# Transpositions of q and k as 64-row tiles, half-size loads, and a new instruction order in an attention and gated-MLP kernel

## The chip, the cores and the metric

The kernel runs on one core of a Trainium2 chip. The metric is the device time in microseconds. Three runs of the kernel before took 740.59, 742.3 and 740.95 us; the median is 740.95 us. Smaller is better.

The engines are TensorE (PE, its weight loads shown apart as PEld), VectorE (DVE), ScalarE (ACT), GpSimd (POOL) and SyncE (SP, which here issues nearly all DMAs). A line number such as L526 is a line of the kernel before.

## What is computed

An attention with hashed buckets, followed by a gated MLP with a spatial gate. Everything is float32.

```python
B, H, S, D = q.shape                       # 4, 8, 768, 64
q_bits = (einsum('bhsd,dk->bhsk', q, proj) > 0)        # 6 bits each, for q and k
mask = q_bucket[:, :, :, None] == k_bucket[:, :, None, :]
scores = where(mask, scale * q @ k.T, -1e9)
attn = exp(scores - max(scores)); attn /= sum(attn) + 1e-9
x = (attn @ v) as (B, S, H*D)              # 4 x 768 x 512
h = gelu(x @ w_in)                         # 512 -> 1024
u, v = halves of h;  v_n = layernorm(v) * g_ln
v_s = w_sg @ v_n + b_sg                    # 768 x 768 over positions
out = x + (u * v_s) @ w_out
```

## The kernel before, in words

Two heads of one batch form a pair; there are 16 pairs. The attention of a pair is done with both heads side by side on the 128 partitions: head 0 on partitions 0 to 63, head 1 on 64 to 127. For that q and k must stand transposed, with the 64 features on the partitions and the 768 positions along the row.

For each pair the work is this:

- `load` (L502) issues, from SP's queue, two DMAs for q and two for k, one for each head, 192 KB each. They put 128 positions on the partitions, in six blocks. The tiles `q` and `k` have one buffer each, so a pair's load waits until the pair before has been read.
- `parts` (L519) transposes: `tr` (L523) makes six TensorE transpositions of 128x128 into two PSUM banks for q, and six for k. ScalarE copies the result back over the same tile (L536), makes the rounded high part `hq`, `hk` (L530), and VectorE the low part `lq`, `lk` (L533).
- `features` (L546) projects q and k on the six hash vectors (L553). VectorE takes the signs (`fc`, L556), and four DMAs from SP (L569) scatter them into `fq` and `fk`.
- `largest` (L573) computes, for six tiles of queries, approximate masked scores in 24 pairs of matmuls (L584), and VectorE takes the row maxima (L589). `shift` (L592) spreads the maxima with three small matmuls (L602) and writes them into `fq` (L608).
- `weigh` (L612) computes the exact scores, four terms each (L624), and ScalarE takes the exponential `p` (L629). GpSimd adds the exponentials up (L642).
- `weighted` (L645) multiplies by v (L654), and sums the denominators (L678).

The matmuls of L584 and L624 take 64 rows and 128 columns each, two at a time: one head on the upper 64 rows of the array, the other on the lower. The transpositions take all 128 rows.

The second part of the program, the gated MLP (L845, L876, L894, L923), comes after the last pair. Beside the attention run the conversion of its weights (L379 to L389) and other preparations.

The order of all instructions is set by the class `Plan`. Every piece of work is added with an engine, a cost and a priority (`add`, L99), and `order` (L129) plays a list schedule with these numbers. The priorities come from constants at the top (L22 to L49). Each engine then runs its list strictly in that order. `form` tells the planner which shape the array has for a piece; `TURN_PE` is what it charges for a change of shape.

Of the kernel before, what the change touches and what calls it, by code (L numbers as in the profile page):

```python
# [14 lines left out]
AF = mybir.ActivationFunctionType  # L15
ALU = mybir.AluOpType
# [5 lines left out]
MLP = {"xl": "POOL", "gm": "DVE", "gl": "POOL", "wg": 450.84, "wo": 131.34, "x": 480}  # L22
# [3 lines left out]
HID = 308.55  # L26
AVP = 3.07
S0P = -1.32
AHEAD = 4
PREP, SHIFTP, FINP, WSTEP, WP = 8.92, -3.65, 6.26, 37.69, 29.58  # L30
LOADS = "SP"
GPLACE = 4
XLATE = 7.75
FEAT = 2.17
LOWP = 7.32
LOADP = -0.4
LATF = 3.2
# [11 lines left out]
ADDW = 1  # L49


class Plan:
# [23 lines left out]
    def __init__(self):  # L76
        self.groups, self.tags = [], {}
# [21 lines left out]
    def add(self, engine, cost, prio, fn, r=(), w=(), dma=0, port=None, form=None, lat=0.0):  # L99

        port = engine == "POOL" if port is None else port
        g = {"e": engine, "c": cost, "p": prio, "fn": fn, "dma": dma, "n": len(self.groups), "slots": [], "port": port, "form": form, "lat": lat}
# [163 lines left out]
def kernel(  # L266
# [190 lines left out]
    if True:  # L457
# [44 lines left out]
        def load(n, prio):  # L502
# [16 lines left out]
        def parts(st, s, prio):  # L519
# [15 lines left out]
            plan.add(PE, 0.654, prio, tr, [raw], [tp])  # L535
            plan.add(ACT, 0.81, prio, lambda: nc.scalar.copy(x_of(raw).rearrange("p (a b) -> p a b", a=2), tp()[:, :, :SH]), [tp], [raw])  # L536
            def split(p1, p2):
                plan.add(ACT, 0.81, p1 + OH[s], high, [raw], [hh])
                plan.add(DVE, 0.98, p2 + OL[s], low, [raw, hh], [lo], port=True)
# [6 lines left out]
        def features(st, prio, merged=False):  # L546
# [13 lines left out]
            else:  # L560
                plan.add(PE, 0.66, prio, project, st.raw, [fp], form="col32")
            st.sign = lambda prio: plan.add(DVE, 0.56, prio, sign, [fp], [fc])
# [10 lines left out]
        def largest(st, t, prio):  # L573
# [13 lines left out]
            for kh in range(2):  # L587
                plan.add(PE, 0.346, prio + 0.01 * kh + OM[2 * t + kh], lambda kh=kh: mm(kh), [*st.hi, *st.ft], [sc[kh]], form="row")
                plan.add(DVE, 0.95, prio + OM[2 * t + kh], lambda kh=kh: nc.vector.tensor_reduce(  # L589
                    mx()[:, i, :, kh], sc[kh]()[:, :, :SH], axis=AX.X, op=ALU.max, negate=True), [sc[kh]], [(mx, (kh, i))])  # L590

        def shift(st, hf, prio):  # L592
# [5 lines left out]
                m()[:, :, MROW::BL], mx(), axis=AX.X, op=ALU.min), [mx], [m])  # L598
# [5 lines left out]
            plan.add(PE, 0.18, prio, spread, [m], [tp])  # L604
            ft, cs = st.ft[0], slice(hf * SH, (hf + 1) * SH)
            for b in range(2):
                r = b * BL + MROW
                plan.add(ACT, 0.47, prio, lambda r=r: nc.scalar.copy(ft()[r:r + 1, cs], tp()[r:r + 1, :SH]), [tp], [(ft, hf)])  # L608
# [3 lines left out]
        def weigh(st, hf, k0, prio):  # L612
# [13 lines left out]
            for i, kt in enumerate(kts):  # L626
                plan.add(PE, 0.692, prio + 0.01 * i + OW[HT * 2 * hf + kt], lambda i=i: mm(i), [qh, ql, kh, kl, kf, (qf, hf)], [sc[i]], form="row")
                ticks.append(plan.buf("tick", 1000))
                plan.add(ACT, 0.81, prio, lambda i=i: nc.scalar.activation(p[i]()[:, :, :SH], sc[i]()[:, :, :SH], AF.Exp),  # L629
                         [sc[i]], [p[i], ticks[-1]])  # L630

            st.p += p
            for i, kt in enumerate(kts):
# [6 lines left out]
                else:  # L640
                    for j in range(2):
                        plan.add(POOL, 1.03, prio + 0.6, lambda i=i, j=j, first=first: nc.gpsimd.tensor_add(  # L642
                            sums()[:, j], (first or sums)()[:, j, :SH], p[i]()[:, j, :SH]), [p[i]] + ([first] if first else []), [(sums, j)])

        def weighted(st, hf, prio, owed, nxt=None):  # L645
# [12 lines left out]
            else:  # L658
# [8 lines left out]
                plan.add(PE, 1.3 * HT, prio - 0.01, product, p + [v_], [av], form="col")  # L667
# [318 lines left out]
```

## Time and profile before

| | |
|---|---|
| median of three runs | 740.95 us |
| profiled execution, its own time | 739.75 us |
| span of the profiled execution | 738.0 us |
| PE busy | 717.1 us (97%) |
| DVE busy | 544.0 us (74%) |
| POOL busy | 459.8 us (62%) |
| ACT busy | 379.5 us (51%) |

The page counts a matmul as busy from its start to its modelled end. Matmuls overlap, so busy time of PE says little on how full it is; the steps from one start to the next say more. The attention takes the span from about 25 to 426 us, the gated MLP the rest.

### The profile page before, as it was taken

Reading aid. Unit: us, or ns where it says so; the run is one execution under the profiler, and the core shown is the slowest. Engines: PE = TensorE matmul, PEld = TensorE weight load, DVE = VectorE, ACT = ScalarE, POOL = GpSimd, SP = SyncE. Lnnn points to the kernel's source line nnn. Section 1 sums busy time; section 2 is a strip of 40 time slices with the busy share of each in tenths; the row PEclk is TensorE's granted clock in tenths of the full one; section 3 lists DMA queues with packets and bytes.
Section 4 is the critical chain, followed back from the end, with each engine's and each line's share of the span. In section 5 each row is a group of like instructions: output and inputs, shape, how many; then the busy total and the mean of one; then the engine's idle time right before and its main releaser. Section 6 shows DMA issues by size and latency. Waiting matters only on the chain.

```text
span 738.0 us, 14443 instructions
## 1 busy us (share of the span) xinstructions
PE 717.1 (97%) x5300; PEld 566.5 (77%) x5300; DVE 544.0 (74%) x859; ACT 379.5 (51%) x623; POOL 459.8 (62%) x465
## 2 busy tenths in 40 slices
PE   6899999999999999999999999999999999999997
PEld 5676676666767666676766669998999889988996
DVE  3887899788898888878788878655864486347733
ACT  3565566665757656565765556530761066106510
POOL 2578889889887878778597976570463045404230
PEclk8999999999999999999999999999999999999999
DMA  6214543653675464255343235935220601061004
GB/s 139 70 45 103 127 114 90 154 132 94 155 143 123 93 149 108 70 128 125 96 108 95 73 85 135 239 68 139 34 64 23 157 15 43 1 147 25 1 1 115
DMA packets 180839, 70.59 MB, mean 96 GB/s; under 512 B 158112, under 2 KB 170528, under 8 KB 180768
## 3 DMA queue, kind: packets, MB, share of 16 engines
q1 hardware_dynamic: 180320, 69.01, 39.3%
q10 hardware_dynamic: 448, 0.66, 0.6%
q8 instruction: 42, 0.69, 0.4%
q14 instruction: 29, 0.24, 0.1%
HBM read 51.61 MB, written 17.24 MB: 93 GB/s over the span
## 4 chain that ended last, share of the span: by engine, by line
PE 76%; DMA 10%; DVE 9%; SPq 2%; issue 2%; ACT 1%; POOL 0%; DVEq 0%; ACTq 0%
PE psb L624 15%; PE psb L654 13%; PE psb L894 11%; PE psb L923 9%; PE psb L845 8%; PE psb L876 7%; PE psb L584 7%; DVE mx L589 4%; DMA r<-sq 2%; PE psb L526 2%; DMA rs<-r 2%; PE psb L678 1%; PE psb L553 1%; DMA sq<-s 1%; PE psb L602 1%
## 5 line engine op out<-in xcount | busy, mean ns | idle before, releaser
L642 POOL TENSOR_TENSOR sum<-sum,p 128x384 f32<-128x384 f32 x256 | 240.7, 977 | 54.8 <-ACT p L629 54.7
L589 DVE TENSOR_REDUCE mx<-psb 128x2 f32<-128x768 f32 x192 | 174.2, 950 | 39.7 <-PE psb L584 39.2
L629 ACT ACTIVATE p<-psb 128x768 f32<-128x768 f32 x192 | 147.1, 815 | 24.3 <-PE psb L624 20.8
L654 PE MATMUL psb<-p,v 128*64 128x385 f32 x768 | 131.2, 491 | 0.0
L654 PEld LDWEIGHTS psb<-p,v 128*64 128x64 f32 x768 | 52.3, 137 | 71.7 <-issue 62.4
L642 POOL TENSOR_TENSOR sum<-p,p 128x384 f32<-128x384 f32 x64 | 71.2, 1133 | 19.5 <-ACT p L629 19.5
L624 PE MATMUL psb<-hq,hk 64*128 64x384 f32 x384 | 72.0, 370 | 5.3 <-DVE mx L589 5.1
L584 PE MATMUL psb<-fk,fq 64*128 64x384 f32 x384 | 68.8, 353 | 2.3 <-DVE mx L589 2.3
L855 POOL TENSOR_TENSOR mv<-mv,epsr 128x1 f32<-128x1 f32 x24 | 13.8, 574 | 86.4 <-DVE mv L854 81.2
L584 PE MATMUL psb<-hk,hq 64*128 64x384 f32 x384 | 66.0, 339 | 0.0
L624 PE MATMUL psb<-lq,hk 64*128 64x384 f32 x384 | 64.9, 333 | 0.0
L624 PE MATMUL psb<-fq,fk 64*128 64x384 f32 x384 | 64.9, 332 | 0.0
L624 PE MATMUL psb<-hq,lk 64*128 64x384 f32 x384 | 64.8, 332 | 0.0
L894 PE MATMUL psb<-wgl,zh 128*128 128x384 f32 x192 | 64.2, 335 | 0.4 <-POOL wgl L817 0.4
L894 PE MATMUL psb<-wgh,zh 128*128 128x384 f32 x192 | 64.1, 334 | 0.0
L894 PE MATMUL psb<-wgh,zl 128*128 128x384 f32 x192 | 64.1, 334 | 0.0
L905 POOL TENSOR_TENSOR gs<-gt,gs 128x384 fp32r<-128x384 f32 x32 | 33.6, 1056 | 48.9 <-ACT gs L902 45.6
L669 ACT COPY un<-psb 128x385 f32<-128x385 f32 x32 | 15.4, 482 | 94.1 <-PE psb L654 94.1
L829 ACT ACTIVATE h<-psb 128x384 f32<-128x384 f32 (+1 forms) x56 | 29.4, 535 | 66.8 <-PE psb L845 59.9
L923 PE MATMUL psb<-woh,gs 128*128 128x512 f32 x192 | 59.9, 389 | 0.0
L897 DVE TENSOR_TENSOR gt<-psb,b_bc 128x384 f32<-128x384 f32 x32 | 17.8, 556 | 46.3 <-PE psb L894 43.5
L624 PEld LDWEIGHTS psb<-hq,hk 64*128 64x128 f32 x384 | 36.1, 184 | 16.8 <-DVE mx L589 11.3
(111 smaller groups left out, 1576.4 us busy)
## 6 DMA issues: line engine op xcount, KB each, us to landing
q<-in_q_dram SPq DMA_DIRECT2D x32, 192.0 KB, 4.3
k<-in_k_dram SPq DMA_DIRECT2D x32, 192.0 KB, 3.6
v<-in_v_dram SPq DMA_DIRECT2D x16, 384.0 KB
rs<-r SPq DMA_DIRECT2D x64, 96.0 KB, 3.0
xs<-xt SPq DMA_DIRECT2D x32, 192.0 KB, 3.3
x<-xs SPq DMA_DIRECT2D x16, 384.0 KB, 3.5
rx<-xs SPq DMA_DIRECT2D x96, 64.0 KB, 2.3
out_dram<-ob SPq DMA_DIRECT2D x24, 256.0 KB, 2.3
```

The costliest lines, as they stand in the source:

```text
L584: nc.tensor.matmul(sc[kh]()[:, j, :SH], x[0]()[row(j), qs], x[1]()[row(j), kh * SH:(kh + 1) * SH], start=(n == 0), stop=(n == 1))
L589: plan.add(DVE, 0.95, prio + OM[2 * t + kh], lambda kh=kh: nc.vector.tensor_reduce(mx()[:, i, :, kh], sc[kh]()[:, :, :SH], axis=AX.X, op=A ...
L624: nc.tensor.matmul(sc[i]()[:, j, :SH], x()[row(j), ks], y()[row(j), cs], start=(n == 0), stop=(n == 3))
L629: plan.add(ACT, 0.81, prio, lambda i=i: nc.scalar.activation(p[i]()[:, :, :SH], sc[i]()[:, :, :SH], AF.Exp), [sc[i]], [p[i], ticks[-1]])
L642: plan.add(POOL, 1.03, prio + 0.6, lambda i=i, j=j, first=first: nc.gpsimd.tensor_add(sums()[:, j], (first or sums)()[:, j, :SH], p[i]()[: ...
L654: nc.tensor.matmul(av()[row(j), :SH + 1], v_()[:, j, kt, :], p[kt]()[:, j, :], start=(kt == 0), stop=(kt == NT - 1))
L829: plan.add(ACT, ua - 0.02, prio, lambda: nc.scalar.activation(h2()[:, :n], ps()[:, :n], AF.Square), [ps], [h2])
L845: nc.tensor.matmul(ps(), x()[:, ts_], w[:, c, FH:FF], start=(c == 0 and n == 0), stop=(c == NC - 1 and n == 2))
L876: nc.tensor.matmul(ps()[:, :SH], w[:, c, fs], x()[:, cs], start=(c == 0 and n == 0), stop=(c == NC - 1 and n == 2))
L894: nc.tensor.matmul(vp()[:, :SH], z()[:, t, fs], w()[:, t, cs], start=(t == 0 and n == 0), stop=(t == NT - 1 and n == 2))
L905: nc.gpsimd if e == POOL else nc.vector).tensor_sub(gl()[:, cs], gt(), gh()[:, cs].bitcast(F32)),
L923: nc.tensor.matmul(po(), a()[:, ts_], w()[:, f, :], start=(f == 0 and n == 0), stop=(f == NF - 1 and n == 2))
```

## The change

1. Each load of 192 KB becomes two of 96 KB: positions 0 to 383 go on partitions 0 to 63, positions 384 to 767 on partitions 64 to 127. A pair's q and k take eight DMAs where they took four.
2. The transposition of q (and of k) becomes twelve of 64 rows where it was six of 128 rows. Each takes a block of 64 positions by 128 columns. Those of partitions 0 to 63 write one PSUM bank, those of partitions 64 to 127 the other, alternating. The planner is told cost 0.35 and form "row" for them, where it was 0.654 and no form.
3. The planner gets a table `SHAPE` of small offsets to priorities, by a tag of the piece of work and its number, and other constants. The order of the instructions on all engines is drawn anew with them.

No matmul, reduction or vector operation is added or left out otherwise; the shapes of all other instructions stay.

```diff
-MLP = {"xl": "POOL", "gm": "DVE", "gl": "POOL", "wg": 450.84, "wo": 131.34, "x": 480}
+MLP = {"xl": "POOL", "gm": "DVE", "gl": "POOL", "wg": 461.58, "wo": 124.51, "x": 480}
-HID = 308.55
+HID = 281.5
...
+SHAPE = {"A": [0.0, 0.0, 0.0, -1.0, 0.0, ...
...
+        if tag in SHAPE:
+            i = self.count[tag] = self.count.get(tag, -1) + 1
+            prio += SHAPE[tag][i % len(SHAPE[tag])]
...
                 for j in range(2):
-                    def fn(eng, t=t, j=j, src=src):
-                        eng.dma_start(t()[:, :, j, :], src[st.b, 2 * st.hp + j].rearrange("(t p) d -> p t d", t=NT))
-                    dma(prio + 0.2 * s, 1.09, fn, w=[(t, j)], e=LOADS)
+                    for r in range(2):
+                        def fn(eng, t=t, j=j, r=r, src=src):
+                            eng.dma_start(t()[row(r), :, j, :],
+                                          src[st.b, 2 * st.hp + j, r * SH:(r + 1) * SH].rearrange("(t c) d -> c t d", c=D))
+                        dma(prio + 0.2 * s, 0.55, fn, w=[(t, (j, r))], e=LOADS)
...
             def tr():
-                for hf in range(2):
-                    for i in range(HT):
-                        nc.tensor.transpose(tp()[:, hf, i * P:(i + 1) * P],
-                                            raw()[:, hf * HT + i].rearrange("p j d -> p (j d)"), ident)
+                for t in range(NT):
+                    for r in range(2):
+                        nc.tensor.transpose(tp()[:, r, t * D:(t + 1) * D],
+                                            raw()[row(r), t].rearrange("p j d -> p (j d)"), ident[row(r), row(r)])
...
-            plan.add(PE, 0.654, prio, tr, [raw], [tp])
+            plan.add(PE, 0.35, prio, tr, [raw], [tp], form="row", tag="T")
```

`row(j)` is `slice(64 * j, 64 * j + 64)`. The other added lines only hand a tag to `plan.add`.

The order is shown at three places. The line numbers of the changed kernel are larger: L534 there is L526 before, L561 is L553, L592 is L584, L610 is L602, L632 is L624; on SP L517 is L510, L727 is L719, L577 is L569; on VectorE L541 is L533, L564 is L556, L597 is L589, L605 is L597. A row joins equal instructions that follow each other.

First, PE in the middle of the attention of pair 0, at the transpositions for pair 2 (`k_358` and `q_393` before, `k_439` and `q_391` now). Before:

```order
L584 MATMUL psb<-hk_0_343,hq_0_308 128x384 x2
L526 MATMUL psb<-ident,k_358 128x128 x6
L526 MATMUL psb<-ident,q_393 128x128 x6
L624 MATMUL psb<-hq_0_262,hk_0_273 128x384 x2
L624 MATMUL psb<-hq_0_262,lk_0_283 128x384 x2
```

Now:

```order
L592 MATMUL psb<-hk_0_380,hq_0_373 128x384 x2
L534 MATMUL psb<-ident,k_439 128x64 x12
L534 MATMUL psb<-ident,q_391 128x64 x12
L632 MATMUL psb<-hq_0_272,hk_0_289 128x384 x2
L632 MATMUL psb<-hq_0_272,lk_0_299 128x384 x2
```

The place between the two kinds of score matmuls is the same; twelve narrow transpositions stand where six wide ones stood.

Second, PE in the opening, from the transpositions of pair 0 (`q_249`) to the projections of pair 1 (`q_285` and `k_294` before, `q_301` and `k_312` now). Before, with ten rows of L584 left out in the middle:

```order
L526 MATMUL psb<-ident,k_252 128x128 x6
L553 MATMUL psb<-q_249,pw 32x384 x2
L553 MATMUL psb<-k_252,pw 32x384 x2
L526 MATMUL psb<-ident,q_285 128x128 x6
L584 MATMUL psb<-fk_170,fq_169 128x384 x2
L584 MATMUL psb<-hk_0_273,hq_0_262 128x384 x2
...
L526 MATMUL psb<-ident,k_294 128x128 x6
L553 MATMUL psb<-q_285,pw 32x384 x2
L553 MATMUL psb<-k_294,pw 32x384 x2
L602 MATMUL psb<-identr,m_71 66x128 x3
```

Now:

```order
L534 MATMUL psb<-ident,k_254 128x64 x12
L561 MATMUL psb<-q_249,pw 32x384 x2
L561 MATMUL psb<-k_254,pw 32x384 x2
L592 MATMUL psb<-fk_170,fq_169 128x384 x2
L592 MATMUL psb<-hk_0_289,hq_0_272 128x384 x2
...
L534 MATMUL psb<-ident,k_312 128x64 x12
L534 MATMUL psb<-ident,q_301 128x64 x12
L561 MATMUL psb<-q_301,pw 32x384 x2
L561 MATMUL psb<-k_312,pw 32x384 x2
L610 MATMUL psb<-identr,m_71 66x128 x3
```

The transposition of pair 1's q moved from ahead of the first twelve pairs of score matmuls to behind them, beside that of k.

Third, SP's queue at the start of the program. Before:

```order
L510 DMA q_249<-in_q_dram 128x6x64 x2
L510 DMA k_252<-in_k_dram 128x6x64 x2
L719 DMA v_279<-in_v_dram 128x12x64
L719 DMA v_281<-in_v_dram 128x12x64
L510 DMA q_285<-in_q_dram 128x6x64 x2
L569 DMA fq_169<-fc_288 32x384 x2
L569 DMA fk_170<-fc_288 32x384 x2
L510 DMA k_294<-in_k_dram 128x6x64 x2
```

Now:

```order
L517 DMA q_249<-in_q_dram 64x6x64 x4
L517 DMA k_254<-in_k_dram 64x6x64 x4
L727 DMA v_295<-in_v_dram 128x12x64
L727 DMA v_297<-in_v_dram 128x12x64
L517 DMA q_301<-in_q_dram 64x6x64 x2
L577 DMA fq_169<-fc_303 32x384 x2
L577 DMA fk_170<-fc_303 32x384 x2
L517 DMA q_301<-in_q_dram 64x6x64 x2
L517 DMA k_312<-in_k_dram 64x6x64 x4
```

The kinds follow each other as before, with twice the loads of q and k; half of pair 1's q moved behind the scatter of pair 0's signs.

## Rows read from the trace of the kernel before

**Rows 1.** The page: the span.
```profile
span 738.0 us, 14443 instructions
```

**Rows 2.** Busy time by stretch, attention and MLP; columns as in the first line.
```profile
core 0: us, PE busy (x) PEld busy (x) DVE busy (x) ACT busy (x) POOL busy (x), PEclk, DMA share, GB/s
26.00:420.00 394.00, 386.53 (x3565) 272.29 (x3563) 336.82 (x469) 245.16 (x391) 324.79 (x332) 1.00 0.47 111
426.00:738.00 312.00, 307.12 (x1582) 277.07 (x1580) 187.56 (x341) 123.11 (x218) 124.19 (x109) 1.00 0.32 76
```

**Rows 3.** Timeline of PE around pair 3's transpositions: start us, us, instruction.
```profile
67.95 0.33 PE L584 MATMUL psb<-fk,fq 64*128 64x384 f32 x2
68.12 0.34 PE L584 MATMUL psb<-hk,hq 64*128 64x384 f32 x2
68.39 0.88 PE L526 MATMUL psb<-ident,k 128*128 128x128 f32 x6
69.10 0.82 PE L526 MATMUL psb<-ident,q 128*128 128x128 f32 x6
69.85 0.44 PE L624 MATMUL psb<-hq,hk 64*128 64x384 f32 x2
70.13 0.34 PE L624 MATMUL psb<-hq,lk 64*128 64x384 f32 x2
```

**Rows 4.** Weight loads of q's transpositions, by source line: ns min/median/max, first and last start.
```profile
L526 PEld LDWEIGHTS psb<-ident,q x96: 137/140/230, 5.5 to 380.6; 128*128 128x128 f32 x96
```

**Rows 5.** Timeline of PEld at both ends of that transposition.
```profile
68.39 0.20 PEld L526 LDWEIGHTS psb<-ident,k 128*128 128x128 f32 x2 [0.25 <-ACT p L629]
...
69.85 0.19 PEld L624 LDWEIGHTS psb<-hq,hk 64*128 64x128 f32 x2 [0.17 <-DVE xt L703]
69.96 0.19 PEld L624 LDWEIGHTS psb<-hq,lk 64*128 64x128 f32 x2
```

**Rows 6.** Timeline of PE, projections of 384 columns.
```profile
74.67 0.49 PE L553 MATMUL psb<-q,pw 128*32 128x384 f32 x2
75.00 0.49 PE L553 MATMUL psb<-q,pw 128*32 128x384 f32 x2
```

**Rows 7.** Waits of PEld and PE, 26 to 420 us: us in total, times, longest.
```profile
PEld psb L624 <- DVE mx L589: 9.6, 22, 1.3
PEld psb L584 <- DVE mx L589: 5.4, 15, 2.1
...
PE psb L624 <- DVE mx L589: 4.0, 7, 1.0
PE psb L584 <- DVE mx L589: 2.3, 3, 1.8
```

**Rows 8.** Timeline of PE behind pair 6's transpositions.
```profile
147.43 0.45 PE L624 MATMUL psb<-hq,hk 64*128 64x384 f32 x2 [1.02 <-DVE mx L589]
```

**Rows 9.** Timeline of SP's queue in the opening.
```profile
0.73 1.03 SPq L510 DMA_DIRECT2D q<-in_q_dram  x2
...
13.91 1.11 SPq L510 DMA_DIRECT2D k<-in_k_dram  x2
```

**Rows 10.** The chain that ended last, in the opening: start us, us, what.
```profile
19.80 0.81 ACT k L536
...
23.06 0.74 DVE lq L533
...
23.84 0.96 DVE mx L589
...
24.85 1.85 PE psb L624 x13
```

**Rows 11.** Timeline of SP: the last load for pair 4.
```profile
84.67 0.44 SPq L510 DMA_DIRECT2D k<-in_k_dram  x1
```

**Rows 12.** Timeline of PE: the transposition of that k.
```profile
93.72 0.55 PE L526 MATMUL psb<-ident,k 128*128 128x128 f32 x3
```

**Rows 13.** The page: issues of k by SP, KB each, median us to landing.
```profile
k<-in_k_dram SPq DMA_DIRECT2D x32, 192.0 KB, 3.6
```

More of the change, by code (lines that the diff above doesn't have):

```diff
@@ L76, in __init__ @@
     def __init__(self):
-        self.groups, self.tags = [], {}
+        self.groups, self.tags, self.count = [], {}, {}
     def buf(self, tag, bufs, make=None, need=None):
@@ L97, in place, with add @@
         return min((max(s[i], t), -s[i ^ 1], -s[i], i) for i in s)[0::3]
[L99 removed]
+    def add(self, engine, cost, prio, fn, r=(), w=(), dma=0, port=None, form=None, lat=0.0, tag=None):
         port = engine == "POOL" if port is None else port
[L102 removed]
+        if tag in SHAPE:
+            i = self.count[tag] = self.count.get(tag, -1) + 1
+            prio += SHAPE[tag][i % len(SHAPE[tag])]
+        g = {"e": engine, "c": cost, "p": prio, "fn": fn, "dma": dma, "n": len(self.groups), "slots": [], "port": port, "form": form, "lat": lat, "tag": tag}
         deps, after = set(), set()
@@ L560, in features @@
             else:
-                plan.add(PE, 0.66, prio, project, st.raw, [fp], form="col32")
-            st.sign = lambda prio: plan.add(DVE, 0.56, prio, sign, [fp], [fc])
+                plan.add(PE, 0.66, prio, project, st.raw, [fp], form="col32", tag="F")
+            st.sign = lambda prio: plan.add(DVE, 0.56, prio, sign, [fp], [fc], tag="sg")
             st.fc = fc
@@ L587, in largest @@
             for kh in range(2):
-                plan.add(PE, 0.346, prio + 0.01 * kh + OM[2 * t + kh], lambda kh=kh: mm(kh), [*st.hi, *st.ft], [sc[kh]], form="row")
+                plan.add(PE, 0.346, prio + 0.01 * kh + OM[2 * t + kh], lambda kh=kh: mm(kh), [*st.hi, *st.ft], [sc[kh]], form="row", tag="M")
                 plan.add(DVE, 0.95, prio + OM[2 * t + kh], lambda kh=kh: nc.vector.tensor_reduce(
-                    mx()[:, i, :, kh], sc[kh]()[:, :, :SH], axis=AX.X, op=ALU.max, negate=True), [sc[kh]], [(mx, (kh, i))])
+                    mx()[:, i, :, kh], sc[kh]()[:, :, :SH], axis=AX.X, op=ALU.max, negate=True), [sc[kh]], [(mx, (kh, i))], tag="R")
         def shift(st, hf, prio):
@@ L607, in shift @@
                 r = b * BL + MROW
-                plan.add(ACT, 0.47, prio, lambda r=r: nc.scalar.copy(ft()[r:r + 1, cs], tp()[r:r + 1, :SH]), [tp], [(ft, hf)])
+                plan.add(ACT, 0.47, prio, lambda r=r: nc.scalar.copy(ft()[r:r + 1, cs], tp()[r:r + 1, :SH]), [tp], [(ft, hf)], tag="C")
         ticks = []
@@ L626, in weigh @@
             for i, kt in enumerate(kts):
-                plan.add(PE, 0.692, prio + 0.01 * i + OW[HT * 2 * hf + kt], lambda i=i: mm(i), [qh, ql, kh, kl, kf, (qf, hf)], [sc[i]], form="row")
+                plan.add(PE, 0.692, prio + 0.01 * i + OW[HT * 2 * hf + kt], lambda i=i: mm(i), [qh, ql, kh, kl, kf, (qf, hf)], [sc[i]], form="row", tag="W")
                 ticks.append(plan.buf("tick", 1000))
                 plan.add(ACT, 0.81, prio, lambda i=i: nc.scalar.activation(p[i]()[:, :, :SH], sc[i]()[:, :, :SH], AF.Exp),
-                         [sc[i]], [p[i], ticks[-1]])
+                         [sc[i]], [p[i], ticks[-1]], tag="E")
             st.p += p
@@ L642, in weigh @@
                         plan.add(POOL, 1.03, prio + 0.6, lambda i=i, j=j, first=first: nc.gpsimd.tensor_add(
-                            sums()[:, j], (first or sums)()[:, j, :SH], p[i]()[:, j, :SH]), [p[i]] + ([first] if first else []), [(sums, j)])
+                            sums()[:, j], (first or sums)()[:, j, :SH], p[i]()[:, j, :SH]), [p[i]] + ([first] if first else []), [(sums, j)], tag="A")
         def weighted(st, hf, prio, owed, nxt=None):
@@ L666, in weighted @@
                 plan.add(PE, 0.35 + (0.66 if nxt else 0.0), prio - 0.02, sumup, p[-1:] + [sums] + (nxt.raw if nxt else []), [tp] + ([nxt.fp] if nxt else []), form="col32")
-                plan.add(PE, 1.3 * HT, prio - 0.01, product, p + [v_], [av], form="col")
+                plan.add(PE, 1.3 * HT, prio - 0.01, product, p + [v_], [av], form="col", tag="AV")
             half.un = un = late.ring([P, SH + 1], F32, "un", 4)
-            plan.add(ACT, 0.48, prio - 1, lambda: nc.scalar.copy(un(), av()[:, :SH + 1]), [av], [un])
+            plan.add(ACT, 0.48, prio - 1, lambda: nc.scalar.copy(un(), av()[:, :SH + 1]), [av], [un], tag="un")
             if owed is not None:
```

31 lines of the change are left out of this document (16 added, 15 removed).

## The prediction

> **What bounds the kernel now.** I read the page first for the span [rows 1], then busy time by stretch [rows 2], then PE's timeline around one place where the change acts [rows 3], and last who PE waits for [rows 7]. The granted clock is 1.00, that is 2.4 GHz, in both stretches [rows 2], so the time of PE's work is that of its instructions. In the attention, what the reader is to see is the step from one start to the next: 68.12 less 67.95 is 0.17 us for one pair of score matmuls [rows 3], and such steps follow each other nearly without a gap. PE's waits for VectorE's maxima add up to 9.6 + 5.4 + 4.0 + 2.3 = 21.3 us of 394 [rows 7], some 5%. So PE's own work bounds the attention, and work taken off PE there should shorten it. VectorE is the next: 336.82 us busy of 394, 85%; GpSimd has 324.79, 82% [rows 2]. The MLP behind has the same instructions as before and fills PE [rows 2]; I cost it at no change, give or take 1 us for the moved preparations of its weights.
>
> **What the transpositions cost now.** From the start of the last pair of L584 ahead of them, 68.12, to the start of the second pair of L624 behind them, 70.13, are 2.01 us [rows 3]. Two steps of score matmuls without transpositions would take 2 x 0.17 = 0.35 us. So the twelve transpositions of a pair cost 1.66 us. They consist of: the first weight load, 0.06 (k's row is 0.88 long, q's 0.82, with the same six steps); twelve steps, six of which go from 68.39 to 69.10 with that load in them, so 0.65 for six, 0.11 each, 1.30 for twelve; a gap ahead, 68.12 + 0.17 = 68.29 to 68.39, 0.10; a gap behind, to 69.85, about 0.10; and the first load of L624, not hidden, 69.85 to 69.96 = 0.11 [rows 3, 5].
>
> **What they cost after.** The trace shows no transposition of 64 rows, so I bound it. A step has two parts that overlap: the stream of columns and the next weight load.
>
> The stream: float32 takes 75.00 - 74.67 = 0.33 us for 384 columns [rows 6], 0.86 ns a column, and the present transposition 0.11 for 128, the same. 64 columns take 0.055. Two of them, on the two halves of the array, run side by side, as the score matmuls do (two in 0.17).
>
> The load: two loads in a row of a present transposition span 0.20 [rows 5], one takes 0.14 [rows 4]. So the second starts 0.06 after the first, and the 0.06 that k's row is longer agrees: 128 columns are loaded in 0.06. The loads of the two 64-row halves start together: two in 0.19, where the next two start 0.11 later [rows 5].
>
> So two transpositions take max(0.055, 0.06) = 0.06, and twelve such steps for q and k 0.72 us. The array then has the same two 64-row tiles before, during and after, so I take the gaps and the first load as gone, and of L624's load 0.05 as not covered by the short last step; and 0.09 for waits that lay behind them. That is 0.86, against 1.66: 0.80 saved in a pair. If both gaps and the loads stay, it is 1.07 and the saving 0.59; without the 0.09, 0.89. There are 16 pairs; those of pairs 0 and 1 lie in the opening. For 14 pairs the sum is 14 x 0.80 = 11.2 us, 8.3 to 12.5.
>
> The Trainium skill ("TensorE: Matmul & The Clock Gate", section "LDWEIGHTS (loading the stationary operand)") speaks against this: a weight load takes as long as its columns at 1.2 GHz, and 32 rows take no less than 128. By that a load of 128 columns is 107 ns, an estimate from that page, and it would bound the step instead of the stream. The row of the present transposition, 0.06, disagrees; that of the score matmuls, 0.11, agrees. Which holds for the new shape is the first rival below.
>
> **What is queued differently.** Four more DMAs in each pair, at about 0.5 us of SP (1.03 for two [rows 9]), are 2 us more of SP's time. In the running attention this is hidden: the last load for pair 4 is issued at 84.67 [rows 11], lands some 3.6 us later [rows 13], and is used at 93.72 [rows 12]; 5.4 us are to spare. If the cover goes, PE waits only for what exceeds 5.4. I cost it at nothing.
>
> In the opening it is not hidden. Before, k of pair 1 is issued at 13.91 [rows 9], its copy ends at 20.6, and the chain goes over VectorE's low part and the maxima to the first exact scores at 24.85 [rows 10]. Now six loads stand where two stood, behind the same scatters: 4 x 0.55 = 2.2 us later for the last of them. Of slack there is little: the second load of k is issued from about 14.5, lands 3.6 later [rows 13], some 18.1, and the copy behind the transposition starts at 19.80 [rows 10]. Further, the transposition of q moves beside that of k, so the copy of q (0.81, like that of k [rows 10]) now stands between the last landing and the projection. Up to 3 us can be lost; nothing, if the smaller loads land earlier by as much. I take 2.0, nearer to the rows.
>
> **What is late next.** With 11 us of PE's work gone, VectorE's 336.82 us stand in 383, 88%, and GpSimd's 85%. The idle share of VectorE falls from 14.5 to 12%; if the 21.3 us of waits grow by 14.5/12, that is 4.4 us. On the other side the order is drawn anew for the new costs and may save such waits. I take +1.5, between 0 and 4.4.
>
> **Sum.** -11.2 + 2.0 + 1.5 = -7.7 us against the profiled execution's own 739.75 (span 738.0 and 1.75 around it), so 732.0. That execution lies 1.2 us below the median of the three runs; against the median the forecast is **733 us**. Its own range, with the bounds above, is 728 to 738.
>
> **Rivals.**
>
> First, the new step is bound by weight loads of 0.11 us, both halves side by side. For it: the 64-row loads of L624 take 0.11 [rows 5]. Against: those stand beside 0.17 of streaming and are of another kind of matmul, and the load of the same float32 data takes 0.06. Twelve steps of 0.11 are still 1.30; only the rest goes, the gaps (0.20), the first load (0.06) and half of L624's (0.06), 0.32 in a pair. 14 x 0.32 = 4.5, less 2.0 in the opening and 0.5 of waits: -2, **739**.
>
> Second, the halves do not overlap, and the 24 transpositions follow each other at 0.06. The change then doesn't do what its form says. Against: L624's loads and matmuls do overlap. 24 x 0.06 = 1.44, 0.2 saved in a pair, 2.8 in all, which the opening takes back: **740**. With loads of 0.11 one after the other it would be 2.64 in a pair, 14 x 0.98 + 2.0 more, and 757; I give that 0.02 and count it with the next.
>
> Third, a new stall behind the transpositions, in every pair. Engines run strictly in order, and the score matmuls after them need banks that VectorE's maxima free. For it: one such stall of 1.02 us stands behind pair 6's transpositions [rows 8], PE will be there 0.8 us earlier in each pair, and VectorE has the least room. Against: in most pairs the step is without such a wait, as in rows 3. If all 14 had 1.0 us it would be +14 - 11.2 + 2.0 + 1.0 = +5.8: **747**, slower. It decides from 0.6 us in each pair on, where 14 x 0.6 eats what the rest brings.
>
> Fourth, the new order also takes away waits. A third of the 21.3 us gone instead of 1.5 more: 733 - 1.5 - 7 = **724.5**. For it: pieces that VectorE and PE exchange stand in shorter runs now (the score matmuls behind the transpositions alternate more often with those of the maxima). Against: nothing in the trace shows that those waits come from the order and not from VectorE's load.
>
> **How the numbers follow.** Chances: forecast 0.55, load-bound 0.13, halves one after the other 0.08, stall 0.12, waits removed as well 0.12. A change below 0.2% (1.5 us) can't be told from none. Faster (below 739.5): 0.55 and 0.12 whole, and of the load-bound case 0.09, 0.02 from the others: 0.78. Same: 0.04 + 0.06 = 0.10. Slower: 0.12. For the range I leave out half of the last case below 725 and the stall above 741, with little else: 725 to 741.
>
> **What would show it.** Right: 12 transpositions in pairs of starts some ns apart, steps of 0.06 between pairs, twelve of them in about 0.36; 2.01 us from L584 to L624 becoming 1.2; the period from one pair's transpositions to the next shorter by 0.5 to 0.8; the first exact scores at about 27 instead of 24.85. Load-bound: the same pairs of starts, but steps of 0.11. One after the other: single starts. A stall: idle time of PE ahead of L624 (L632 there) put down to VectorE's maxima, some 1 us each time. If the loads are late, PE's transpositions wait for a DMA of q or k after the opening; that would make my cost of nothing for SP wrong.

## The result and the profile after

The changed kernel takes 745.4 us (median of 20 runs, 741.2 to 749.3) where the kernel before took 740.95 on the same chip; the ratio is 1.0058, with a 95% interval of 1.0043 to 1.0072. It is slower. The forecast was 733, with a range of 725 to 741, so the time lies outside the range and on the other side of no change.

The profiled execution took 747.25 us. By the ratio the kernels are 4.3 us apart (0.58% of 740), so the rows below tell of one execution that is above its median. Its page has the new span, 7.4 us over that of [rows 1]:

```profile
span 745.4 us, 14948 instructions
```

All of it lies in the attention. The first matmul of the MLP starts at 433.8 us of the span instead of 426.4, and from there to the end are 311.6 us in both. The busy times of the attention (columns as in [rows 2], answering to its first row):

```profile
30.00:433.00 403.00, 387.19 (x3769) 274.69 (x3767) 339.33 (x472) 247.80 (x395) 328.65 (x338) 0.99 0.45 109
```

The reader is to see that VectorE, ScalarE and GpSimd have the same work to within a few us, and that it now takes longer to get through it.

PE's timeline at the same transpositions as in [rows 3]:

```profile
70.36 0.34 PE L592 MATMUL psb<-hk,hq 64*128 64x384 f32 x2
70.54 0.54 PE L534 MATMUL psb<-ident,k 64*128 64x64 f32 x12
71.06 0.59 PE L534 MATMUL psb<-ident,q 64*128 64x64 f32 x12
71.46 0.42 PE L632 MATMUL psb<-hq,hk 64*128 64x384 f32 x2
71.72 0.34 PE L632 MATMUL psb<-hq,lk 64*128 64x384 f32 x2
```

From 70.36 to 71.72 are 1.36 us, less two steps of 0.17 is 1.01 (with 0.174 for a step), where it was 1.66. Q's twelve transpositions take 0.40, six steps of 0.067. This part of the change does what the forecast said, at 0.65 a pair.

Then PE's waits for the maxima and for `fq` between 26 and 427 us, answering to [rows 7]:

```profile
PEld psb L632 <- DVE mx L597: 9.3, 16, 2.4
...
PE psb L592 <- ACT fq L616: 5.6, 2, 4.4
PE psb L632 <- DVE mx L597: 5.3, 7, 2.1
...
PEld psb L592 <- DVE mx L597: 1.6, 4, 0.8
...
PE psb L592 <- DVE mx L597: 0.5, 1, 0.5
```

These rows must not be added up as the prediction added [rows 7]. PE and PEld are two views of one engine, and a wait can stand in both: the stall that [rows 8] shows for PE with 1.02 us is this row of PEld, in the kernel before:

```profile
147.43 0.19 PEld L624 LDWEIGHTS psb<-hq,hk 64*128 64x128 f32 x2 [1.26 <-DVE mx L589]
```

Taken apart, the waits for the maxima were 15.0 us on PEld and 6.3 on PE, and are now 10.9 and 5.8. What is new is a wait for `fq`, in two places, of 5.6 us in the rows of PE. The larger of the two leads back through ScalarE to SP. On SP (start us, us, instruction):

```profile
112.21 1.94 SPq L517 DMA_DIRECT2D q<-in_q_dram  x3
114.19 1.96 SPq L517 DMA_DIRECT2D k<-in_k_dram  x3
116.25 1.13 SPq L707 DMA_DIRECT2D r<-sq  x1
117.48 0.38 SPq L378 DMA_DIRECT2D w<-in_moe_w_in_dram  x1
117.91 0.42 SPq L806 DMA_DIRECT2D x<-xs  x1
```

On ScalarE:

```profile
123.75 0.83 ACT L811 CAST xh<-x 128x768 fp32r<-128x768 f32 x1 [8.10 <-DMA x<-xs]
124.49 0.48 ACT L677 COPY un<-psb 128x385 f32<-128x385 f32 x1
124.86 0.94 ACT L616 CAST fq<-psb 1x384 fp32r<-1x384 f32 x2
```

On PE, with the matmuls behind:

```profile
125.86 0.69 PE L592 MATMUL psb<-fk,fq 64*128 64x384 f32 x2 [4.41 <-ACT fq L616]
...
129.49 0.59 PE L592 MATMUL psb<-fk,fq 64*128 64x384 f32 x2
129.81 0.59 PE L592 MATMUL psb<-hk,hq 64*128 64x384 f32 x2
```

The chain reads: six half loads of q and k take SP from 112.21 to 116.15; the load of x, which is the MLP's input and not needed there for 300 us, is issued at 117.91 behind them, and lands only 5.8 us later (before: 110.71 to 114.28, 3.6 us); ScalarE, in its fixed order, stands for 8.10 us at the cast of x; behind the cast stands the write of the maxima into `fq`; PE needs that `fq` and waits 4.41 us. The same chain stands at 96.12 us with a wait of 1.24. In the kernel before, the cast at the same place hardly waited (SP, then ScalarE):

```profile
110.71 0.34 SPq L798 DMA_DIRECT2D x<-xs  x1
...
114.28 0.83 ACT L803 CAST xh<-x 128x768 fp32r<-128x768 f32 x1 [0.65 <-DMA x<-xs]
```

And PE's granted clock fell behind the long wait (columns as in [rows 2]):

```profile
120.00:124.00 4.00, 1.46 (x18) 1.13 (x14) 1.58 (x3) 0.24 (x1) 0.65 (x1) 1.00 0.70 206
...
126.00:128.00 2.00, 2.00 (x27) 1.67 (x29) 1.02 (x2) 1.59 (x3) 1.68 (x3) 0.50 0.00 0
128.00:130.00 2.00, 2.00 (x19) 2.00 (x18) 1.13 (x2) 1.25 (x2) 1.92 (x3) 0.50 0.05 17
```

After 4.41 us of idleness the clock is 0.50, that is 1.2 GHz, until about 131 us; a step of score matmuls takes 0.32 instead of 0.17. Those 5 us do some 2.5 us of work.

The opening: SP's loads for pair 1, as in [rows 9], and PE:

```profile
16.04 1.35 SPq L517 DMA_DIRECT2D q<-in_q_dram  x2
17.49 2.60 SPq L517 DMA_DIRECT2D k<-in_k_dram  x4
```

```profile
22.08 0.56 PE L534 MATMUL psb<-ident,k 64*128 64x64 f32 x11 [0.25 <-DMA k<-in_k_dram]
...
28.46 0.44 PE L632 MATMUL psb<-hq,hk 64*128 64x384 f32 x2 [0.24 <-DVE mx L597]
```

The first exact scores start at 28.46 instead of 24.85 [rows 10], 3.6 us late. Of these, 2.0 are there before pair 1: the first score matmuls start at 16.81 instead of 14.81, since the loads of pair 0 are doubled too and the last transpositions of its k wait for them until 8.73 (before: 6.75). The other 1.6 come behind the loads of pair 1's k.

### The profile page after: what moved, and what is told of

Its sections match the earlier page's. It is cut to its first block, busy times and chain, and to the rows that moved or that the text cites. A ratio compares the mean times of both kernels' runs of the same rounds, so it can differ in the third digit from the quotient of the medians.

```text
span 745.4 us, 14948 instructions
## 1 busy us (share of the span) xinstructions
PE 712.0 (96%) x5492; PEld 565.5 (76%) x5492; DVE 543.0 (73%) x859; ACT 380.0 (51%) x623; POOL 457.6 (61%) x465
## 4 chain that ended last, share of the span: by engine, by line
PE 60%; DVE 8%; DMA 7%; SPq 4%; issue 2%; ACT 1%; POOL 1%; DVEq 0%; ACTq 0%
PE psb L902 11%; PE psb L632 10%; PE psb L931 9%; PE psb L662 9%; PE psb L853 7%; PE psb L884 7%; PE psb L592 4%; DVE mx L597 3%; DMA sq<-s 2%; PE psb L686 1%; DMA woh<-wo_h 1%; SPq L517 1%; SPq L709 1%; PE psb L561 1%; SPq L777 1%
## 5 line engine op out<-in xcount | busy, mean ns | idle before, releaser
L650 POOL TENSOR_TENSOR sum<-sum,p 128x384 f32<-128x384 f32 x256 | 244.5, 981 | 55.8 <-ACT p L637 51.0
L597 DVE TENSOR_REDUCE mx<-psb 128x2 f32<-128x768 f32 x192 | 174.9, 949 | 39.3 <-PE psb L592 38.5
L637 ACT ACTIVATE p<-psb 128x768 f32<-128x768 f32 x192 | 148.8, 813 | 26.4 <-PE psb L632 22.5
L592 PE MATMUL psb<-fk,fq 64*128 64x384 f32 x384 | 69.2, 351 | 11.8 <-ACT fq L616 5.6
L632 PE MATMUL psb<-hq,hk 64*128 64x384 f32 x384 | 73.2, 373 | 5.5 <-DVE mx L597 5.3
L592 PE MATMUL psb<-hk,hq 64*128 64x384 f32 x384 | 67.7, 343 | 0.0
L632 PE MATMUL psb<-hq,lk 64*128 64x384 f32 x384 | 65.8, 334 | 0.0
L632 PE MATMUL psb<-fq,fk 64*128 64x384 f32 x384 | 65.7, 334 | 0.0
L632 PE MATMUL psb<-lq,hk 64*128 64x384 f32 x384 | 65.7, 334 | 0.0
L592 PEld LDWEIGHTS psb<-fk,fq 64*128 64x128 f32 x384 | 38.4, 190 | 16.9 <-ACT fq L616 6.3
```

What stands on the lines that cost most here:

```text
L592: nc.tensor.matmul(sc[kh]()[:, j, :SH], x[0]()[row(j), qs], x[1]()[row(j), kh * SH:(kh + 1) * SH], start=(n == 0), stop=(n == 1))
L632: nc.tensor.matmul(sc[i]()[:, j, :SH], x()[row(j), ks], y()[row(j), cs], start=(n == 0), stop=(n == 3))
```

## The experiments

All ratios are to the kernel before, run on the same chip.

**The change taken apart.** Five kernels hold the order of one kernel and exchange loads or transpositions. With whole loads the copy behind the 64-row transpositions puts the positions in order (`a` is the half, `c` the position in a block):

```diff
-nc.scalar.copy(x_of(raw).rearrange("p (a b) -> p a b", a=2), tp()[:, :, :SH])
+nc.scalar.copy(x_of(raw).rearrange("p (t a c) -> p a t c", a=2, c=D),
+               tp()[:, :, :SH].rearrange("p a (t c) -> p a t c", c=D))
```

The changed kernel's order and 64-row transpositions, whole loads:

```diff
                     for r in range(2):
...
-                            eng.dma_start(t()[row(r), :, j, :], ...
+                            if r == 0:
+                                eng.dma_start(t()[:, :, j, :], src[st.b, 2 * st.hp + j].rearrange("(t p) d -> p t d", t=NT))
```

> The changed kernel's order and 64-row transpositions, but each load of a head is one DMA of 192 KB again (issued where the first half stood); ScalarE's copy puts the 64-position blocks in order. Theory S (the doubled loads do the harm: SP issues late, and engines that run in order stand behind transfers): at least 8 us faster than the changed kernel, 733 to 738, and first exact scores near 25 us. Theory O (the new order does the harm): within 3 us of the changed kernel's 745. Theory D (VectorE and GpSimd take back what PE saves, whatever the order): 740 to 743.

Measured: 734.5 us, 0.9956 [0.9931, 0.9981].

The kernel before with half loads (the positions lie in the tile as before), transpositions of 128 rows:

```diff
-                        eng.dma_start(t()[:, :, j, :], ...
+                        for r in range(2):
+                            eng.dma_start(t()[row(r), :, j, :], ...
```

> The kernel before with one thing changed: each load of a head is issued as two DMAs of 64 partitions, one behind the other; the positions lie in the tile as before, and the transpositions are the old ones. Theory S: slower than before by 6 to 12 us, of it some 3 in the opening. Theory O: within 2 us of before. Theory D: within 2 us.

Measured: 762.5 us, 1.0323 [1.0294, 1.0352].

The kernel before with 64-row transpositions, whole loads (the `tr` of the change, and the copy above):

```diff
-                for hf in range(2):
-                    for i in range(HT):
+                for t in range(NT):
+                    for r in range(2):
...
```

> The kernel before with whole loads and its own order, only the transpositions in twelve of 64 rows. Theory S and theory O: 7 to 11 us faster than before (730 to 734), since PE's 0.8 us in each of 14 pairs come through. Theory D: 0 to 3 us faster, with PE's waits for VectorE's maxima up by about what its work went down.

Measured: 736.9 us, 0.9974 [0.9957, 0.9991].

The kernel before with both, loads and `tr` as in the change:

```diff
+                        for r in range(2):
+                            eng.dma_start(t()[row(r), :, j, :], ...
...
+                for t in range(NT):
+                    for r in range(2):
...
```

> The kernel before's order with both parts of the change, half loads (each pair of halves issued together) and 64-row transpositions. Theory S: 740 to 747, as the changed kernel. Theory O: 730 to 734. Theory D: 738 to 741.

Measured: 760.2 us, 1.0304 [1.0272, 1.0336].

The changed kernel's order alone: whole loads, 128 rows:

```diff
-                for t in range(NT):
-                    for r in range(2):
+                for hf in range(2):
+                    for i in range(HT):
...
+                            if r == 0:
+                                eng.dma_start(t()[:, :, j, :], ...
```

> The changed kernel's order alone: whole loads (one DMA where the first half stood) and the old transpositions of 128 rows. With whole loads the new order and the 64-row transpositions together were 0.44% faster than before, the 64-row transpositions in the old order 0.26%. If the new order is good by itself: 738 to 740 against before's 738.4, and the 64-row transpositions are worth 4 to 6 us in it. If the new order brought all of the gain: 735 to 736.

Measured: 741.3 us, 1.0025 [1.0006, 1.0044].

What follows: the transpositions are worth 0.26% in the old order and, from 1.0025 to 0.9956, 0.69% in the new one. The new order alone gains nothing. The half loads lose: 3.2% in the old order, and from 0.9956 to 1.0058, 1.0% in the new. The whole loss is theirs.

**Why the transpositions bring so little in the old order.** Rows of PE's waits for the maxima, 26 to 420 us, in the kernel before with 64-row transpositions:

```profile
PEld psb L624 <- DVE mx L589: 12.9, 28, 1.5
PE psb L624 <- DVE mx L589: 5.8, 13, 1.4
PEld psb L584 <- DVE mx L589: 5.8, 14, 1.5
PE psb L584 <- DVE mx L589: 1.8, 4, 1.2
```

On PEld they are 18.7 against 15.0 [rows 7], on PE 7.6 against 6.3: between 1.3 and 3.7 us of what the transpositions free come back as waits for VectorE's maxima. To test whether VectorE stands in the way, three of the seven VectorE operations of each weight conversion (L379 to L389) are left out, in that kernel and in the kernel before:

```diff
-vec(lambda: sts(xf(), g(), LEAST * LEAST, xf(), op0=ALU.is_ge, op1=ALU.mult), [x, g], [x])
+vec(lambda: None, [x, g], [x])
...
```

> The old order with 64-row transpositions and whole loads, and with three of VectorE's seven operations in each conversion of weights left out (L383, L386, L387: about 2.1 us in each of 24 jobs, some 50 us; the converted weights are then other numbers). To be compared with the next. Theory D (VectorE stands in the way of PE's saving): 7 to 10 us faster than the next kernel. Otherwise: 1 to 3 us faster, as without the omission.

> The kernel before with the same three VectorE operations of each weight conversion left out. Theory D: faster than before by 3 to 8 us, less than the one before this gains by the same omission. Otherwise: within 3 us of before.

Measured: 729.6 us, 0.9880 [0.9867, 0.9892], with the transpositions, and 736.6 us, 0.9976 [0.9962, 0.9989], without. With VectorE relieved the transpositions are worth 0.96%, 7.1 us, instead of 0.26%. VectorE's work is what stood next. The omission shortens the weight conversions too, so it doesn't show that the maxima alone are what was late.

**What it is in the half loads.** First, the mere place in the queue, in the old order: a DMA of 64 times 4 bytes, which nobody reads, behind each load.

```diff
                         eng.dma_start(t()[:, :, j, :], ...
+                        eng.dma_start(scratch[row(j), 2 * n + s:2 * n + s + 1], src[st.b, 2 * st.hp + j, :D, 0:1])
```

> The kernel before with whole loads, and behind each load of q or k one more DMA of 64 elements of 4 bytes into a scratch tile that nothing reads: SP issues as many DMAs as with half loads, the data and their layout stay. Theory Q (what costs is the place that the added DMAs take in SP's queue): 15 to 25 us slower than before, as with the half loads in this order. Theory L (what costs is the half-size transfers, on 64 partitions): within 3 us of before.

Measured: 747.7 us, 1.0134 [1.0104, 1.0165]. This lies between the two theories: ten of the 24 us that half loads cost in that order.

Then the opening (pairs 0 and 1) and the running attention apart; `whole` is `n < 2` in the first kernel and `n >= 2` in the second, both in the changed kernel's order:

```diff
+                            if not whole:
                                 eng.dma_start(t()[row(r), :, j, :], ...
+                            elif r == 0:
+                                eng.dma_start(t()[:, :, j, :], ...
```

> The changed kernel, its order kept, but q and k of pairs 0 and 1 come in whole loads; pairs 2 to 15 keep the half loads. Measured so far against the kernel before: the changed kernel 1.0058, the same with whole loads everywhere 0.9956, 7.5 us apart. Theory S (the doubled loads hold up SP's queue all through the attention): only the opening's part returns, the 3.6 us by which the first exact scores were late, so a ratio near 1.001 (741 us where before takes 740). Rival O (what was lost in the opening is the loss; the running attention hides the loads): nearly all returns, 0.996 to 0.997 (737 us).

> The changed kernel, its order kept, half loads for pairs 0 and 1 only; whole loads for pairs 2 to 15. Theory S: 0.9956 and 3.6 us of 740 more, 1.0005. Rival O: as slow as the changed kernel, 1.005 to 1.006.

The third is the kernel before, with half loads for pairs 2 to 15:

```diff
+                        if n < 2:
                             eng.dma_start(t()[:, :, j, :], ...
+                        for r in range(2 if n >= 2 else 0):
+                            eng.dma_start(t()[row(r), :, j, :], ...
```

> The kernel before, its order and its transpositions, with half loads for pairs 2 to 15 and whole loads for pairs 0 and 1. With half loads everywhere it had 1.0323. Theory S: less the 3.7 us by which the first exact scores were late there, 1.027. Rival O: 1.005 or less.

Measured: 740.3 us, 1.0016 [0.9999, 1.0032], with half loads in the running attention alone; 736.2 us, 0.9966 [0.9953, 0.9980], in the opening alone; 758.3 us, 1.0258 [1.0236, 1.0281], in the old order. The running part costs 0.60% (from 0.9956 to 1.0016). The opening costs 0.10% beside whole loads and 0.42% beside half loads (1.0016 to 1.0058): alone, most of the 2.9 us by which the first exact scores were late (28.22 and 25.32) were made up later. The rival by which only the opening loses is out.

**The changed kernel planned for whole loads.** As the first kernel, but the planner knows one load for each head and draws the order from it:

```diff
-                    for r in range(2):
-                        ...
-                        dma(prio + 0.2 * s, 0.55, fn, w=[(t, (j, r))], e=LOADS)
+                        dma(prio + 0.2 * s, 1.09, fn, w=[(t, j)], e=LOADS)
```

> The changed kernel with whole loads that the planner knows of (one DMA of cost 1.09 for each head, as before), 64-row transpositions and the copy that puts the positions in order; everything else of its constants kept, and the order drawn from them. Theory S: no slower than the same with the order kept, 0.9956, give or take 0.4% by which a new order alone moves the time: 0.991 to 1.000. Rival (the constants were drawn for half loads, and fit nothing else): above 1.000.

Measured: 759.6 us, 1.0290 [1.0272, 1.0308]. A miss of theory S: two of the periods from one pair's transpositions to the next, some 25 us elsewhere, are 32.4 and 35.3. The constants suit one set of costs; with another the order can be 3% worse.

**Queue or transfers.** In the changed kernel's order: second halves of pairs 2 to 15 issued by GpSimd, or by ScalarE; or whole loads, with a small DMA where the second half stood.

```diff
+                            eng = nc.gpsimd if r and n >= 2 else eng
                             eng.dma_start(t()[row(r), :, j, :], ...
```

> The changed kernel, its order kept, but for pairs 2 to 15 the second half of each load is issued by GpSimd and not by SP, so that SP issues as many loads as in the kernel before and the transfers are the changed kernel's. Theory S (what costs is the place in SP's queue): the running part returns and the opening's stays, 0.997 to 1.000, if GpSimd, which waits 60 us in the attention for other things, has the room. Rival H (half-size transfers into 64 partitions are what costs, whichever queue they are in): as the changed kernel, 1.005 to 1.007.

```diff
+                            eng = nc.scalar if r and n >= 2 else eng
                             eng.dma_start(t()[row(r), :, j, :], ...
```

> The same with ScalarE issuing the second halves. ScalarE issues in order among its copies and exponentials, so 56 issues of about 0.6 us are 34 us of an engine that is busy half of the time. Theory S: between 0.997 and 1.003, below the changed kernel's 1.0058. Rival H: 1.006 or more.

```diff
+                            if r == 0:
+                                eng.dma_start(t()[:, :, j, :], ...
+                            elif n >= 2:
+                                eng.dma_start(scratch[row(j), 2 * n + s:2 * n + s + 1], src[st.b, 2 * st.hp + j, :D, 0:1])
```

> The changed kernel's order and 64-row transpositions with whole loads; in the place where pairs 2 to 15 would issue the second half of a load, a DMA of 64 times 4 bytes into a tile that nobody reads. It has the changed kernel's number of issues on SP in the running attention, without half-size transfers. Without the small DMAs it had 0.9956; with half loads in pairs 2 to 15 alone, 1.0016. Theory S: most of those 0.60% appear, 0.999 to 1.002. Rival H: 0.995 to 0.997.

Measured: 781.6 us, 1.0574 [1.0550, 1.0597], with GpSimd; 745.1 us, 1.0085 [1.0069, 1.0100], with ScalarE; 735.0 us, 0.9950 [0.9933, 0.9966], with small DMAs. By these the theory that each further issue costs would fall, and half-size transfers would be the cause. But the first two put new work and new waits in place of the old. GpSimd's rows show 28.5 us of waits ahead of its loads of q, most of it in one:

```profile
L518 POOL DMA_DIRECT2D q<-in_q_dram x28: 648/668/859, 26.1 to 411.6; - x28
...
26.06 1.52 POOL L518 DMA_DIRECT2D q<-in_q_dram  x2 [19.24 <-PE psb L611]
```

That one costs little: GpSimd has nothing to add up before 31.25 in any case. But the other 9.3 us have the sums behind them, and the 56 issues of about 0.66 us are 37 us more (an estimate from these rows) for an engine that was busy for 328.65 of 403. So this run doesn't part queue from transfers.

With ScalarE, one new wait of PE, 2.34 us at 64.51 for `p`, stands in a period of 30 us. And x comes at different times. From the start of the scatter into `fq` to the issue of x are 9.61 us with whole loads (99.68 to 109.29), 10.60 with small DMAs (100.58 to 111.18), 12.47 with half loads (103.98 to 116.45, opening whole). To the cast, for which x must have landed, they are 16.46 us (to 116.14), 15.86 (to 116.44) and 17.43 (to 121.41). PE's longest waits for `fq` go by the landing: 2.04 us, 1.64 and 3.04. The waits of two of these runs (start us, us). With small DMAs:

```profile
91.54 0.45 PE L595 MATMUL psb<-fk,fq 64*128 64x384 f32 x2 [0.69 <-ACT fq L619]
118.55 0.44 PE L595 MATMUL psb<-fk,fq 64*128 64x384 f32 x2 [1.64 <-ACT fq L619]
```

With half loads in pairs 2 to 15:

```profile
93.74 0.45 PE L595 MATMUL psb<-fk,fq 64*128 64x384 f32 x2 [1.87 <-ACT fq L619]
123.51 0.44 PE L595 MATMUL psb<-fk,fq 64*128 64x384 f32 x2 [3.04 <-ACT fq L619]
```

Each of the two waits is longer with half loads, 4.9 us in all against 2.3. So a third theory was formed: what matters is neither the number of issues nor the size of the transfers by itself, but how late x comes.

**The load of x taken out of the queue.** The one edit, in the changed kernel, in its order with whole loads, and in the kernel before as control (`b` is the batch; the four loads of batch 0 are moved):

```diff
-lambda eng, x=x, c=c: eng.dma_start(x(), xs[b][c * P:(c + 1) * P, :])
+lambda eng, x=x, c=c: (eng if b else nc.scalar).dma_start(x(), xs[b][c * P:(c + 1) * P, :])
```

> The changed kernel, its order kept, with one edit: the four loads of x during the attention are issued by ScalarE, at their place in its own order, instead of by SP behind the doubled loads. Theory X (the running part of the loss is mostly two chains: half loads ahead of x in SP's queue, ScalarE waiting for x, its writes of the maxima into fq behind that, TensorE waiting 1.24 and 4.41 us for them): TensorE's two waits for fq shrink to under 1 us each, and the ratio falls from 1.0058 to between 0.998 and 1.002. Rival S (the doubled loads cost a little at many places): 1.004 or more, with the period from the transpositions at 97 us to the next staying near 29 us.

> The changed kernel's order and 64-row transpositions with whole loads (0.9956), and the four loads of x issued by ScalarE. It still had one TensorE wait of 2.04 us for fq behind x. Theory X: that goes, 0.993 to 0.995. Rival S: 0.995 to 0.997.

> The kernel before with its loads of x issued by ScalarE, as a control. Before, no wait of TensorE for fq of 0.4 us or more stands between 64 and 130 us of the span. Theory X: 0.998 to 1.002. If moving these loads is good by itself wherever they stand: 0.997 or less.

Measured: the changed kernel 735.8 us, 0.9968 [0.9953, 0.9983]; with whole loads 730.2 us, 0.9904 [0.9871, 0.9937]; the control 739.4 us, 1.0017 [1.0002, 1.0031]. Four DMAs on another queue, and the changed kernel goes from slower to faster than the kernel before, by 0.9%, more than I expected. The same edit does nothing for the kernel before. ScalarE in the changed kernel with x moved:

```profile
112.66 0.33 ACTq L806 DMA_DIRECT2D x<-xs  x1
...
116.59 0.83 ACT L811 CAST xh<-x 128x768 fp32r<-128x768 f32 x1 [2.12 <-DMA x<-xs]
...
118.44 0.94 ACT L616 CAST fq<-psb 1x384 fp32r<-1x384 f32 x2
```

and PE there:

```profile
120.11 0.33 PE L592 MATMUL psb<-fk,fq 64*128 64x384 f32 x2
120.28 0.34 PE L592 MATMUL psb<-hk,hq 64*128 64x384 f32 x2
120.45 0.54 PE L534 MATMUL psb<-ident,k 64*128 64x64 f32 x12
```

`fq` is written by 119.4, and PE goes through in steps of 0.17 where it stood 4.41 us. The transpositions of that pair start at 120.45 instead of 126.70. VectorE's wait for `w` there stays (4.56 us before the edit, 3.01 with it), so that wait is not what held PE. The version with whole loads beats both kernels: of those that do the whole work it is the fastest here.

The edit does two things to x. In the changed kernel x is issued 17.13 us behind the start of the transpositions before it (95.53 to 112.66) instead of 20.95 (96.96 to 117.91), and it lands in 3.9 us instead of 5.8. With whole loads the issue hardly moves (17.40 us behind those transpositions, 16.73 with the edit), and nearly all of the gain is the landing, 6.85 us before (SP, then ScalarE):

```profile
109.29 0.38 SPq L806 DMA_DIRECT2D x<-xs  x1
...
116.14 0.83 ACT L811 CAST xh<-x 128x768 fp32r<-128x768 f32 x1 [5.74 <-DMA x<-xs]
```

and 4.06 with the edit (108.97 to 113.03). On SP's queue x stood right behind the 256 KB of `w`, on ScalarE's it was issued ahead of them; which of the two, the other queue or the place ahead of `w`, made it land sooner is not shown.

The Trainium skill ("DMA: Bandwidth & Descriptors", section "Issuing engines are not separate DMA queues") says that issuing from several engines saves only the time of the sequencer, usually little beside the DMA. The runs here disagree: on SP those four issues took 0.42 to 1.45 us, 3.5 in all, on ScalarE 0.33 each, yet moving them brought 0.9%, 6.6 us. What was saved is, beyond their own time, the wait behind half loads, the slower landing, and what stood behind these. The run with GpSimd shows the other side: an issue that must wait holds up the engine that it is on (the 9.3 us above).

## Why the prediction was wrong

**The step that failed: "In the running attention this is hidden ... I cost it at nothing."** For the load of q and k itself that was nearly right. The sign that the prediction named for it, transpositions that wait for q or k after the opening, stands in the trace in one place with 0.4 us. With x moved, the changed kernel's span is 4.0 us above that of the same with whole loads (732.1 and 728.1), and 3.3 of these are there at the first exact scores (28.91 and 25.61). But the cover was worked out for the loads' own reader, PE at 93.72 [rows 12], and not for what stands behind them in SP's queue. The next rows of SP should have been followed to their readers: x, then ScalarE, then `fq`, then PE. It cost 1.24 + 4.41 us of PE and about 2.5 us of half clock, 8.1 us. Three things joined: half loads ahead of x; the new order, which put x behind the loads of `r` and `w` too; and the slower landing behind them. With whole loads that order still had one such wait, of 2.04 us at 118.25.

**"So two transpositions take ... 0.06 ... 0.80 saved in a pair."** The mechanism was right, the size a little off: 0.65, inside the bounds of 0.59 to 0.89; 14 pairs are 9.1 us instead of 11.2. The steps are 0.067, with starts in pairs, and the rival bound by weight loads of 0.11 did not come. By the Trainium skill's rule ("TensorE: Matmul & The Clock Gate", section "LDWEIGHTS (loading the stationary operand)") a load of 128 columns would have bounded a step at 107 ns, an estimate from that page; the trace disagrees, as the row before had said.

**"I take 2.0" in the opening.** It was 3.6. What it counted, the six loads behind the scatters, came out near: 1.6 us, though they take SP 1.35 + 2.60 = 3.95, 0.66 each and not 0.55. What it left out is that pair 0's own loads are doubled, ahead of the scatters: 2.0 us.

**"I take +1.5" for what is late next.** VectorE was rightly named, but the 21.3 us behind the bound of 4.4 count waits twice, once for PE and once for its weight loads. In the old order the waits rose by 3.7 us on PEld and 1.3 on PE; yet of the 9.1 us that the transpositions free there only 1.9 (0.26%) came through, so more was lost behind VectorE than these rows hold. In the new order they fell by 4.1 and 0.5. At 285.31 a transposition itself waits 1.88 us for a bank, the third rival's kind of stall, but not in every pair.

The sum by what was measured. From the first exact scores to the MLP, the columns as in [rows 2], before and now:

```profile
24.85:426.40 401.55, 394.08 (x3621) 276.89 (x3621) 342.93 (x475) 248.06 (x396) 331.19 (x338) 1.00 0.46 110
...
28.46:433.80 405.34, 389.53 (x3790) 276.53 (x3790) 341.67 (x473) 249.12 (x396) 329.45 (x339) 0.99 0.45 109
```

These are 3.8 us more; with the 3.6 of the opening that is the 7.4 of the span. PE's idle time, length less busy time, went from 7.5 to 15.8, 8.3 more. 5.6 of that are the two waits for `fq`. The next largest is a wait of 2.09 us for the maxima at 235.72, with a clock of 0.59 in the four us behind, which costs some 1.6 more. With the 2.5 behind the wait of 4.41, the half clock cost 4.1. PE's busy time fell by 4.5, so by 8.6 without the half clock, near the 9.1 of the transpositions. 8.3 + 4.1 - 8.6 is the 3.8.

The wait at 235.72 is a chain of the same kind, with another DMA (SP, VectorE, PE):

```profile
228.13 1.37 SPq L806 DMA_DIRECT2D x<-xs  x1
229.60 1.14 SPq L709 DMA_DIRECT2D rs<-r  x2
231.17 0.33 SPq L704 DMA_DIRECT2D sq<-s  x1
...
234.63 0.19 DVE L705 RECIPROCAL sq<-sq 128x6 f32<-128x6 f32 x1 [3.01 <-DMA sq<-s]
234.74 1.79 DVE L597 TENSOR_REDUCE mx<-psb 128x2 f32<-128x768 f32 x2
...
235.72 0.45 PE L632 MATMUL psb<-hq,hk 64*128 64x384 f32 x2 [2.09 <-DVE mx L597]
```

VectorE stands for 3.01 us at the reciprocal of the sums, with the maxima behind it, for a DMA that is issued behind x and two loads of `rs`. With x moved VectorE waits 0.86 us at that place, PE for none, and the same stretch, from the transpositions at 126.7 (there 120.45) to the MLP, is 5.3 us shorter. Why `sq` came that late is not shown step by step.

Why half loads cost as much as 24 us in the old order was not settled: 4.8 lie in the opening (1.0323 and 1.0258 of 738), and VectorE's and GpSimd's waits for the loads of weights grew from 5.5 and 6.3 us to 12.0 and 11.6 (28 to 430 us).

## What to carry to other kernels

Before you call a DMA hidden, follow what stands behind it in its queue: each of those has a reader, and on an engine that runs in order a reader of something that isn't urgent can hold up the one instruction that is. A load that others depend on, late in a queue, may go to another queue, but not to an engine that has no room for the issues or where they have to wait with work behind them. And when work is taken off the engine that bounds, price the next engine's waits from a run in which that engine is relieved; here it decided between 0.26 and 0.96%.

## What was not expected of the hardware

- Cutting a load in two doubles what it costs SP, and more: a whole load of 192 KB took 0.53 to 0.54 us to issue (median, kernel before), a half load of 96 KB into 64 partitions 0.62 to 0.63, a DMA of 64 times 4 bytes 0.55. By these medians the size hardly matters to the issuing engine.
- A wait of 4.41 us on PE was followed by about 5 us at a clock of 0.50, one of 2.09 by four us at 0.59; such a wait cost half as much again or more.
- The same load of 384 KB, the second of x, landed 3.9 to 4.1 us after its issue in the two kernels that issue it on ScalarE, and 5.0 to 6.9 us after its issue in four that issue it on SP behind a load of weights.
- Two 64-row float32 transpositions on the two halves of the array take 0.067 us together, with no gap of 0.10 to the score matmuls ahead, whose tiles have the same shape.
